# Attention with two mixture layers on one core: v in chunks of 128 tokens, a dummy exponential at the start, and a newly derived order

## The chip, the cores and the metric

The kernel runs on one core of a Trainium2 chip. The metric is device microseconds of that core from the first to the last instruction, beside what lies around them. Five engines matter: TensorE (PE in the profile; PEld is its weight loads), VectorE (DVE), ScalarE (ACT), GpSimd (POOL) and SyncE (SP), which here issues every DMA. Each engine works through its own instructions in the order in which they were written.

## The reference, cut to what matters

```python
# q, k, v: (4 batches, 8 heads, 576 tokens, 64); p: (4, 8, 32, 64)
def sm_attn(qq, kk, vv):
    s = 0.125 * qq @ kk.T
    a = exp(s - max(s)); a = a / (sum(a) + 1e-9)
    return a @ vv
pp  = sm_attn(p, k, v)          # 32 packed rows per head
x   = sm_attn(q, pp, pp)        # back to 576 tokens; heads joined: (2304, 512)
h   = x @ w_in                  # first MoE: 512 -> 2048
x   = (h * cos(h)) @ w_out      # 2048 -> 512
out = sum over 4 experts e of share[:, e] * (relu(x @ w1[e]) @ w2[e])   # second MoE: 512 -> 1024 -> 512
```

## The kernel before

**Stages.** For each of four batches `attn_p` computes the packed attention: scores (`f_s1`, helper line 353), maximum and exponential (L377 to L386), six transposes of the exponentials in chunks of 96 tokens (`f_tr`, L392), a copy of them out of the accumulators (`f_aT`, L396), and the product with v (`f_pv`, L409), for each of two halves `e` of the heads. `attn_q` computes the second scores (`f_s2`, again helper line 353), transposes them on DVE (L466), takes maxima (L470), exponentials (L477) and sums, and writes the result in two parts, rounded (`f_hi`, L499) and remainder (`f_lo`, L658), as tile `at`. `w_block` decodes 64-bit weights: load, absolute value on ACT (L264), clamp, shift and sign on DVE (L271, L275, L280), low word on ACT (L285), sum on POOL (L294). `m_front` (helper line 353, then L547) folds the packed attention into the first weight matrix; `a_front` (products on L205 to L207, cosine on L573 to L590) and `a_back` are the first MoE, in 16 steps of one batch and one quarter of its 2048 columns. The second MoE takes the tokens in thirds, eight steps each; for the last two thirds `b_back2` forms seven products a step, collects them in sums (L1134), and after a third's last step adds the sums into each other (`final`, L1149) and stores them (`put`, L1156). Every product is three matmuls of a rounded part and a remainder (`mm3`, L205 to L207).

**What sets the order.** Nothing is ordered by hand. `Plan` is a small list planner inside the kernel: each operation has an engine, an assumed cost in us, its predecessors, the buffers that it takes, and a key. `Plan.run` goes through an assumed timeline. Whichever operation can start first is taken next on its engine; among those of one engine that could start at the same moment the smallest key wins; a TensorE operation whose key is more than 60 above the smallest one left is held back. The instructions are written in the resulting order, so a wrong cost does not break anything, but it places an instruction behind one that comes late. The keys stand in the table `KEYS`: for an attention batch `att` (scores, transposes, v product, last transpose, second scores, store), `m`, `f`, `b` for the first MoE, `load` for the loads, `first`, `one`, `two`, `end`, `last` for the second. `last` gives the keys of the seven products of the very last step, in the order of the list `BACK`.

**Costs assumed.** Loads of the first stages are costed at 0.27 MB per us, a half-batch of scores on TensorE at 1.5 us; the first exponential is charged 1.3 us for loading its table. Before the first scores and in planned gaps of the first 31 us TensorE runs matmuls of the identity (L1254, L1365). The loads of one batch pair of v arrive as two tiles of 96 partitions.

Of the kernel before, what the change touches and what calls it, by code (L numbers as in the profile page):

```python
# [26 lines left out]
class Plan:  # L27
# [18 lines left out]
    def op(self, eng, us, f, after=(), take=(), use=(), key=None, table=None, port=False, alt=None, begun=()):  # L46
# [4 lines left out]
        o = {"eng": eng, "us": us, "late": self.late if eng == "SP" else 0.0, "fair": self.late > 0, "f": f, "after": [a for a in after if a is not None], "take": list(take),  # L51
# [11 lines left out]
    def run(self):  # L63
# [4 lines left out]
        port, free, table, taken = 0.0, {}, None, {t: 0 for t in self.bufs}  # L68
# [10 lines left out]
        while done < len(self.ops):  # L79
# [67 lines left out]
def tile_packed_attention_moe_moe2(ctx: ExitStack, tc: tile.TileContext, qT, kT, vk, pT, w_in, w_out, dp, w1, w2, out, out2):  # L147
# [24 lines left out]
    NCH, CH = vk.shape[3], vk.shape[2]  # L172
# [47 lines left out]
    MB = 1 / 0.27  # L220
# [11 lines left out]
    def w_block(what, G, k, key, pieces=1, ld_key=None):  # L232
# [22 lines left out]
        for p in range(pieces):  # L255
# [56 lines left out]
            his.append(h)  # L312
            a = pl.op("POOL", 2.45 * r, f_add, [a, l, h], [], [sraw, sd], key)
# [9 lines left out]
    ld_p = dma(2.5 + 0.26 * MB, lambda: load(ptile, pT), key=-2000)  # L323

    def load_kv(n, vtag, key, key_v):
# [5 lines left out]
        def f_v():  # L331
            p, b, f = (mp, 2, 4) if vtag == "m" else (wo, 4, 4)
# [4 lines left out]
        s["ld_v"] = dma(0.59 * MB, f_v, take=[s["v"]], key=key_v)  # L337

# [17 lines left out]
    def attn_p(bb, keys):  # L356
# [13 lines left out]
        a = pl.op("PE", 1.5, f_s1, [ld_p, u[0]["ld_k"], u[1]["ld_k"]], p1, [u[0]["k"], u[1]["k"]], keys[0])  # L370
        ready = []
        for e in range(2):
# [16 lines left out]
            def f_tr(e=e):  # L389
                s["tpv", e] = tpv = psum2().rearrange("p c n -> p (c n)")  # L390
                for c in range(NCH):
                    nc.tensor.transpose(tpv[:CH, c * P:(c + 1) * P], s["a", e][:, c * CH:(c + 1) * CH], ident)  # L392

            def f_aT(e=e):
                s["aT", e] = aT = dec.tile([P, 2 * 512], F32, tag="T", name="aT", bufs=2)[:CH, :NCH * P]
                nc.scalar.activation(aT, s["tpv", e][:CH, :NCH * P], AF.Copy)  # L396
# [6 lines left out]
            def f_pv(e=e):  # L403
                if e == 0:
                    s["pv"] = psum2()
                for c in range(NCH):
                    for q in range(4):
                        h = 2 * (q % 2) + e
                        nc.tensor.matmul(s["pv"][32 * q:32 * q + 32, e, :64],  # L409
                                         lhsT=s["aT", e][:, c * P + 32 * q:c * P + 32 * q + 32],  # L410
                                         rhs=u[q // 2]["vt"][:, c, 64 * h:64 * h + 64], start=c == 0, stop=c == NCH - 1)
# [11 lines left out]
            b = pl.op("PE", 0.88, f_tr, [x], [p2[e]], [ta], keys[1])  # L423
            b = pl.op("ACT", 0.8, f_aT, [b], [tT], [p2[e]])
            b = pl.op("PE", 0.88, f_pv, [b, u[0]["ld_v"], u[1]["ld_v"]] + ready[-1:], [p3] if e == 0 else [],
# [17 lines left out]
    def attn_q(bb, key, key_st):  # L443
# [12 lines left out]
        first = pl.op("PE", 1.5, f_s2, [un[bb, "ptf"], u[0]["ld_q"], u[1]["ld_q"]], p1, [u[0]["q"], u[1]["q"]], key)  # L456
# [78 lines left out]
    def m_front(G, bb, key):  # L535
# [16 lines left out]
        a = pl.op("PE", 1.25, f_mm, w[0]["ready"] + w[1]["ready"] + [un[bb, "ptf"]], [p1],  # L552
# [546 lines left out]
    def b_back2(n, W, keys):  # L1099
# [4 lines left out]
        for i, (a, b, bank, new, acc, how) in enumerate(BACK):  # L1104
# [22 lines left out]
            def f_evac(ob=ob, ac=ac, acc=acc, how=how, first=first):  # L1127
                p = ob["t"][:, :, :TB]
# [4 lines left out]
                else:  # L1133
                    nc.vector.tensor_tensor(out=ac["t"], in0=ac["t"] if how == ALU.subtract else p,  # L1134
# [7 lines left out]
        if u < NU - 1:  # L1142
            return
# [274 lines left out]
```

## Time and profile before

| | us |
|---|---|
| median of 3 runs (1148.88 to 1152.58) | 1150.12 |
| the profiled execution | 1149.58 |
| its span | 1147.8 |

| engine | busy us | share of the span |
|---|---|---|
| PE | 1101.7 | 96% |
| PEld | 1032.5 | 90% |
| DVE | 835.3 | 73% |
| POOL | 633.2 | 55% |
| ACT | 493.4 | 43% |

The chain of work that ended last is 78% PE, 8% DVE and 5% DMA. An engine that is busy 96% of the span cannot lose much more waiting, so the places to look at are those few where PE waits: a table of stretches shows them. A row of a timeline gives the start in us, the time, the engine, the line, the operation and its tiles, and in brackets how long the engine was idle before it and what ended that.

### The profile page before, as it was taken

What the parts mean: (1) busy time and instruction counts of PE and PEld (TensorE: products, weight loads), DVE (VectorE), ACT (ScalarE), POOL (GpSimd) and SP (SyncE); (2) the same over time, 40 slices, a digit from 0 to 9 for tenths busy, and PEclk for the clock granted to TensorE, in tenths of its full rate; (3) what the DMA queues carried; (4) which work ended last, traced back from release to release, by engine and by line L of the source; (5) the groups of instructions that cost most, each with busy time, mean ns of one, the idle gap of its engine ahead of it and who ended that gap; (6) DMA issues with size and microseconds to landing.
All of it is one profiled execution on the core that took longest, in us unless ns stands there. A gap on an engine that the chain in (4) does not pass through costs nothing.

```text
span 1147.8 us, 19120 instructions
## 1 busy us (share of the span) xinstructions
PE 1101.7 (96%) x7241; PEld 1032.5 (90%) x7241; DVE 835.3 (73%) x1244; ACT 493.4 (43%) x852; POOL 633.2 (55%) x477
## 2 busy tenths in 40 slices
PE   6689999999999999999999999999999999999997
PEld 4568999999999988888888889999999999999997
DVE  3798777567555677787777756888887768778776
ACT  3677655445444453244334434333334343333331
POOL 1454755435422775555566546656667767645553
PEclk8699999999999999999999999999999999999999
DMA  9673436433135859787866967676667876666653
GB/s 314 231 263 118 161 116 266 188 130 141 43 105 188 280 196 325 265 301 256 291 257 263 335 259 249 232 252 233 244 227 249 306 265 238 226 227 219 228 182 110
DMA packets 96815, 257.70 MB, mean 225 GB/s; under 512 B 10892, under 2 KB 34516, under 8 KB 94548
## 3 DMA queue, kind: packets, MB, share of 16 engines
q1 hardware_dynamic: 96724, 256.48, 63.1%
q8 instruction: 57, 0.93, 0.3%
q14 instruction: 34, 0.28, 0.1%
HBM read 192.97 MB, written 71.86 MB: 231 GB/s over the span
## 4 chain that ended last, share of the span: by engine, by line
PE 78%; DVE 8%; DMA 5%; issue 4%; ACT 3%; POOL 2%; SPq 0%; POOLq 0%; ACTq 0%; DVEq 0%
PE pa L205 26%; PE pa L207 25%; PE pa L206 25%; DMA w<-w 3%; PE pa L353 2%; DVE pa L958 1%; DVE s L755 1%; POOL aop L658 1%; POOL w L658 1%; DMA kt<-kT 1%; DVE acc L1134 1%; DVE p L958 1%; DVE u L975 0%; DVE oacc L1077 0%; DVE g L1010 0%
## 5 line engine op out<-in xcount | busy, mean ns | idle before, releaser
L205 PE MATMUL pa<-g,w 128*128 128x288 f32 (+1 forms) x960 | 303.6, 316 | 2.0 <-DVE acc L1134 0.8
L206 PE MATMUL pa<-g,w 128*128 128x288 f32 (+1 forms) x960 | 301.6, 314 | 1.2 <-POOL g L590 1.2
L207 PE MATMUL pa<-g,w 128*128 128x288 f32 (+1 forms) x960 | 301.2, 314 | 0.5 <-POOL w L297 0.5
L658 POOL TENSOR_TENSOR g<-u,g 128x384 fp32r<-128x384 f32 x157 | 171.5, 1105 | 140.3 <-ACT g L667 133.5
L205 PE MATMUL pa<-bop,aop 128*128 128x384 f32 x672 | 228.8, 341 | 9.3 <-DVE p L958 4.1
L207 PE MATMUL pa<-bop,aop 128*128 128x384 f32 x672 | 226.9, 338 | 1.5 <-POOL aop L658 1.5
L206 PE MATMUL pa<-bop,aop 128*128 128x384 f32 x672 | 226.3, 337 | 1.1 <-POOL bop L658 1.1
L205 PEld LDWEIGHTS pa<-g,w 128*128 128x128 f32 x960 | 180.1, 188 | 7.9 <-issue 2.4
L206 PEld LDWEIGHTS pa<-g,w 128*128 128x128 f32 x960 | 180.2, 188 | 1.9 <-POOL g L590 1.9
L207 PEld LDWEIGHTS pa<-g,w 128*128 128x128 f32 x960 | 180.4, 188 | 1.0 <-POOL w L297 1.0
L667 ACT ACTIVATE g<-u 128x384 fp32r<-128x384 f32 x192 | 97.2, 523 | 176.8 <-DVE u L987 134.9
L590 POOL TENSOR_TENSOR g<-t,g 128x576 fp32r<-128x576 f32 x64 | 93.2, 1470 | 118.8 <-ACT g L587 117.4
L205 PEld LDWEIGHTS pa<-bop,aop 128*128 128x128 f32 x672 | 126.1, 188 | 19.1 <-DVE p L958 6.1
L206 PEld LDWEIGHTS pa<-bop,aop 128*128 128x128 f32 x672 | 126.2, 188 | 3.0 <-POOL bop L658 1.4
L207 PEld LDWEIGHTS pa<-bop,aop 128*128 128x128 f32 x672 | 126.1, 188 | 2.2 <-POOL aop L658 2.2
L958 DVE TENSOR_TENSOR p<-pa,p 128x384 f32<-128x384 f32 x144 | 79.3, 554 | 41.4 <-PE pa L207 38.7
L1134 DVE TENSOR_TENSOR acc<-pa,acc 128x768 f32<-128x768 f32 x88 | 83.9, 954 | 32.6 <-PE pa L207 31.3
L658 POOL TENSOR_TENSOR w<-w 128x512 fp32r<-128x512 f32 x62 | 86.3, 1403 | 31.4 <-ACT w L705 31.2
L205 PE MATMUL pa<-at,m 128*128 128x288 f32 x256 | 78.7, 307 | 3.1 <-DVE t L583 2.0
L206 PE MATMUL pa<-at,m 128*128 128x288 f32 x256 | 77.5, 303 | 2.8 <-POOL at L658 2.8
L205 PE MATMUL pa<-w,g 128*128 128x512 f32 x192 | 75.9, 395 | 1.9 <-DVE oacc L1077 1.9
L207 PE MATMUL pa<-at,m 128*128 128x288 f32 x256 | 77.2, 301 | 0.0
(129 smaller groups left out, 1924.8 us busy)
## 6 DMA issues: line engine op xcount, KB each, us to landing
at<-at SPq DMA_DIRECT2D x16, 1152.0 KB, 5.3
raw<-w SPq DMA_DIRECT2D x32, 512.0 KB, 5.2
w<-w SPq DMA_DIRECT2D x64, 256.0 KB, 5.0
raw<-w_in SPq DMA_DIRECT2D x6, 1024.0 KB, 6.1
raw<-w_out SPq DMA_DIRECT2D x6, 1024.0 KB, 8.0
vt<-vk SPq DMA_DIRECT2D x8, 576.0 KB, 8.5
kt<-kT SPq DMA_DIRECT2D x8, 576.0 KB, 10.5
qt<-qT SPq DMA_DIRECT2D x8, 576.0 KB, 8.6
```

Of the source, the lines that this page charges most:

```text
L205: nc.tensor.matmul(o, lhsT=l(0), rhs=r(0), start=first, stop=False, skip_group_check=True)
L206: nc.tensor.matmul(o, lhsT=l(0), rhs=r(1), start=False, stop=False, skip_group_check=True)
L207: nc.tensor.matmul(o, lhsT=l(1), rhs=r(0), start=False, stop=last, skip_group_check=True)
L353: nc.tensor.matmul(o(e)[32 * q:32 * q + 32, :N], lhsT=l[64 * e:64 * e + 64, 32 * q:32 * q + 32], rhs=r(q // 2, q % 2)[64 * e:64 * e + 64], ...
L590: nc.gpsimd.tensor_tensor(out=s["g"][:, 1], in0=s["t"], in1=s["g"][:, 0].bitcast(F32), op=ALU.subtract)
L658: (nc.vector if on_vector else nc.gpsimd).tensor_tensor(out=dst[:, 1], in0=src, in1=dst[:, 0].bitcast(F32), op=ALU.subtract)
L667: nc.scalar.activation(r["t"][:, 0], src(), AF.Copy)
L755: nc.vector.tensor_tensor(out=t, in0=src(a, m)(), in1=src(b, m)(), op=o)
L958: nc.vector.tensor_tensor(out=s[o] if o in s else tmp(o), in0=s[x], in1=s[y], op=ALU.add)
L1134: nc.vector.tensor_tensor(out=ac["t"], in0=ac["t"] if how == ALU.subtract else p, in1=p if how == ALU.subtract else ac["t"], op=how)
```

## The change

The values `v` arrive as four chunks of 128 tokens and a rest of 64 tokens, which both tiles of a batch share, instead of six chunks of 96. An `Exp` activation on a column of zeros is written ahead of the planned work. In the planner the first stages' loads are costed at 0.4 MB per us and scores at 0.85 us, a TensorE operation may follow another without a latency, the exponential's table counts as loaded, loads of later v tiles wait in the plan for `w_out`'s rounding, and the second MoE's work on ACT, DVE and POOL is costed 1.08 times instead of 1.04. All keys are new. In a third's last step of `b_back2` the sums are added with keys that follow product 5 (counted from 0), and product 6 is evacuated and stored in two halves.

```diff
-        port, free, table, taken = 0.0, {}, None, {t: 0 for t in self.bufs}
+        port, free, table, taken = 0.0, {}, "exp", {t: 0 for t in self.bufs}
-            for x, w in [(x, fin) for x in o["next"]] + [(x, t) for x in o["then"]]:
+            for x, w in [(x, t + us if o["fair"] and eng == "PE" == x["eng"] else fin) for x in o["next"]] + [(x, t) for x in o["then"]]:
-    MB = 1 / 0.27
+    MB = 1 / 0.4
...
-            t = p.tile([P, f * 512], F32, tag=vtag, name="vt", bufs=b)[:CH, :NCH * 256]
-            s["vt"] = load(t.rearrange("p (c n) -> p c n", c=NCH), vk[n // 2, n % 2])
+            s["vt"] = t = p.tile([P, 4 * 512], F32, tag=vtag, name="vt", bufs=b)
+            load(t[:, :4 * 256], vk[n // 2, n % 2])
+            if n % 2 == 0:
+                load(t[:64, 4 * 256:6 * 256], vr[n // 2])
...
-        a = pl.op("PE", 1.5, f_s1, [ld_p, u[0]["ld_k"], u[1]["ld_k"]], p1, [u[0]["k"], u[1]["k"]], keys[0])
+        a = pl.op("PE", 0.85, f_s1, [ld_p, u[0]["ld_k"], u[1]["ld_k"]], p1, [u[0]["k"], u[1]["k"]], keys[0])
...
-                for c in range(NCH):
-                    nc.tensor.transpose(tpv[:CH, c * P:(c + 1) * P], s["a", e][:, c * CH:(c + 1) * CH], ident)
+                for c in range(5):
+                    n = P if c < 4 else 64
+                    nc.tensor.transpose(tpv[:n, c * P:(c + 1) * P], s["a", e][:, c * P:c * P + n], ident)
...
-                nc.scalar.activation(aT, s["tpv", e][:CH, :NCH * P], AF.Copy)
+                nc.scalar.activation(aT[:, :4 * P], s["tpv", e][:, :4 * P], AF.Copy)
+                nc.scalar.activation(aT[:64, 4 * P:5 * P], s["tpv", e][:64, 4 * P:5 * P], AF.Copy)
...
+            if u == NU - 1 and i == 6:
+                for d in range(2):
+                    ac["op"] = pl.op("DVE", 0.56, lambda d=d, f=f_evac: f(slice(d, d + 1)), [m, ac["op"]], [],
+                                     [ob["slot"], ac["slot"]], keys[i] + 8)
+                    put(h, acc, 1, 0, keys[i] + 12, d)
+                continue
...
+            if u == NU - 1 and i == 5:
+                final(h, "x74", "v", keys[i] + 9), final(h, "x53", "v", keys[i] + 10)
+                put(h, "x53", 0, 1, keys[i] + 20)
+                final(h, "w", "x53", keys[i] + 11)
+                put(h, "w", 1, 1, keys[i] + 21)
...
-            'in0': [-1061.7, -368.5],
+            'in0': [-1407.6, -625.9],
-            'last': {'b': [39.4, 45.5, 37.7, 357.6, 51.2, 27.5, 165.9]},
+            'last': {'b': [33.4, 24, 67.5, 310.6, 39.6, 16.1, 197.9]},
-            'load': {'in': -1643.2,
+            'load': {'in': -1654.2,
-                     'v3': -1611,
+                     'v3': -1752.6,
-                     'v5': -1628.7,
+                     'v5': -1536.1,
...
+    warm = small.tile([P, 1], F32, tag="mx", name="warm")
+    nc.vector.memset(warm, 0.0)
+    nc.scalar.activation(warm, warm, AF.Exp)
...
-    pl.slow, pl.late = 1.04, 0.8
+    pl.slow, pl.late = 1.08, 0.8
```

## Rows read from the trace of the kernel before

**Rows 1.** Stretches of the span: length, busy us by engine (instructions), TensorE clock, DMA share, GB/s

```profile
0.00:120.00 120.00, 96.20 (x1158) 75.47 (x1159) 85.90 (x174) 73.99 (x114) 50.80 (x42) 0.89 0.66 221
120.00:400.00 280.00, 280.00 (x2173) 268.86 (x2172) 179.72 (x226) 139.54 (x204) 136.98 (x84) 1.00 0.46 164
400.00:600.00 200.00, 193.01 (x954) 170.71 (x954) 149.63 (x219) 81.76 (x159) 121.71 (x83) 1.00 0.75 271
600.00:1141.00 541.00, 532.08 (x2960) 517.29 (x2959) 416.79 (x623) 198.13 (x378) 323.70 (x271) 1.00 0.68 240
```

**Rows 2.** The same table for three parts of the head

```profile
10.00:20.00 10.00, 8.26 (x116) 5.30 (x108) 3.99 (x12) 5.28 (x10) 0.00 (x0) 0.86 1.05 398
...
20.00:60.00 40.00, 25.79 (x334) 17.71 (x334) 28.71 (x61) 24.74 (x44) 19.96 (x15) 0.70 0.75 243
60.00:120.00 60.00, 56.31 (x696) 46.84 (x681) 53.20 (x103) 43.97 (x63) 30.14 (x22) 1.00 0.50 173
```

**Rows 3.** The chain of waits in the first 44 us: start, us, what

```profile
2.59 8.45 DMA kt<-kT
...
22.53 1.74 PE pa L353 x28
```

**Rows 4.** Timeline of ACT from 14 to 24 us

```profile
14.70 1.28 ACT L386 ACT_TABLE_LOAD   x1 [14.70 <-DVE nb L381]
16.00 0.74 ACT L386 ACTIVATE a<-pa,nb 128x576 f32<-128x576 f32 x1
...
22.37 0.69 ACT L264 ACTIVATE wd<-raw 128x512 f32<-128x512 f32 x1
```

**Rows 5.** The tile raw up to 26 us: issues (ns, first and last start), and landing

```profile
L197 SPq DMA_DIRECT2D raw<-w_in x4: 327/380/591, 4.0 to 8.3; - x4
...
DMA to landing us min/median/max: 4.0/10.9/11.8
```

**Rows 6.** Timelines of DVE and PE from 24 to 42 us

```profile
26.91 1.58 DVE L466 STREAM_TRANSPOSE x<-pa 128x288 f32<-128x288 f32 x4 [2.83 <-PE pa L353]
...
29.04 0.41 DVE L271 TENSOR_SCALAR wd<-wd 128x512 f32<-128x512 f32 x1
...
33.49 1.06 PE L353 MATMUL pa<-wd,ptf 64*32 64x512 f32 x2 [5.05 <-POOL wd L294]
...
41.09 0.61 PE L206 MATMUL pa<-at,m 128*128 128x288 f32 x1 [0.61 <-POOL at L658]
```

**Rows 7.** Timeline of ACT from 35 to 40 us

```profile
36.38 0.66 ACT L264 ACTIVATE dt<-raw 128x512 f32<-128x512 f32 x1
...
37.49 0.67 ACT L499 ACTIVATE at<-xt 128x576 fp32r<-128x576 f32 x1
```

**Rows 8.** The chain of waits near 100 us: transposes and v product of one half

```profile
99.59 0.66 PE pa L392 x6
...
101.70 0.81 PE pa L409 x48
```

**Rows 9.** Timeline from 40 to 66 us: copies from accumulators on ACT

```profile
54.21 0.81 ACT L396 ACTIVATE aT<-pa 96x768 f32<-96x768 f32 x1 [0.66 <-PE pa L409]
...
58.20 0.26 ACT L436 ACTIVATE ptf<-pa 128x128 f32<-128x128 f32 x1
```

**Rows 10.** The page's DMA issues: tiles, count, KB each, median us from issue to landing

```profile
at<-at SPq DMA_DIRECT2D x16, 1152.0 KB, 5.3
```

**Rows 11.** PE's waits from 400 to 1141 us, longest in total: us, times, longest

```profile
PE pa L205 <- DVE p L958: 4.8, 9, 1.2
```

**Rows 12.** Timeline of DVE from 1139 us to the end

```profile
1139.40 0.96 DVE L1134 TENSOR_TENSOR acc<-pa,acc 128x768 f32<-128x768 f32 x1 [1.12 <-PE pa L207]
1140.40 0.96 DVE L1149 TENSOR_TENSOR acc<-acc 128x768 f32<-128x768 f32 x1
1141.49 0.96 DVE L1134 TENSOR_TENSOR acc<-pa,acc 128x768 f32<-128x768 f32 x1
1142.48 1.95 DVE L1149 TENSOR_TENSOR acc<-acc 128x768 f32<-128x768 f32 x2
```

More of the change, by code (lines that the diff above doesn't have):

```diff
@@ L50, in op @@
             us, alt = us * self.slow, alt and alt * self.slow
-        o = {"eng": eng, "us": us, "late": self.late if eng == "SP" else 0.0, "fair": self.late > 0, "f": f, "after": [a for a in after if a is not None], "take": list(take),
+        o = {"eng": eng, "us": us, "late": self.late if eng == "SP" else 0.0, "fair": True, "f": f, "after": [a for a in after if a is not None], "take": list(take),
              "use": list(use) + list(take), "key": key, "table": table, "port": port or eng == "POOL", "n": len(self.ops), "next": [],
@@ L146, in tile_packed_attention_moe_moe2 @@
 @with_exitstack
-def tile_packed_attention_moe_moe2(ctx: ExitStack, tc: tile.TileContext, qT, kT, vk, pT, w_in, w_out, dp, w1, w2, out, out2):
+def tile_packed_attention_moe_moe2(ctx: ExitStack, tc: tile.TileContext, qT, kT, vk, vr, pT, w_in, w_out, dp, w1, w2, out, out2):
     nc = tc.nc
@@ L405, in f_pv @@
                     s["pv"] = psum2()
-                for c in range(NCH):
+                for c in range(5):
+                    n = P if c < 4 else 64
                     for q in range(4):
@@ L1161, in b_back2 @@
-        kf = keys[-1] + 20
-        put("c11", 0, 0, kf)
-        final("x53", "v", kf + 1), final("w", "x53", kf + 2), final("x74", "v", kf + 3)
-        put("x53", 0, 1, kf + 10), put("w", 1, 1, kf + 11), put("x74", 1, 0, kf + 12)
+            if u == NU - 1 and i == 2:
+                put(h, "c11", 0, 0, keys[i] + 20)
+            if u == NU - 1 and i == 5:
[3 more added lines that the diff above has]
+                put(h, "w", 1, 1, keys[i] + 21)
@@ new lines, in final, with f, put @@
+    def final(h, x, y, key):
+        a, b = accs[h, x], accs[h, y]
+        def f():
+            nc.vector.tensor_tensor(out=a["t"], in0=a["t"], in1=b["t"], op=ALU.add)
+        a["op"] = pl.op("DVE", 0.95, f, [a["op"], b["op"]], [], [a["slot"], b["slot"]], key, port=True)
+    def put(h, x, i, c, key, d=None):
+        def f():
+            t0 = (h - 1) * TH + c * TB
+            dst = out2[i * 256:(i + 1) * 256, t0:t0 + TB].rearrange("(d p) n -> p d n", p=P)
+            t = accs[h, x]["t"]
+            nc.sync.dma_start(out=dst if d is None else dst[:, d], in_=t if d is None else t[:, d])
+        dma((0.4 if d is None else 0.2) * MB, f, [accs[h, x]["op"]], [], [accs[h, x]["slot"]], key)
@@ L1245, in qq, with kv @@
+    def kv(n, vtag, begun=()):
+        load_kv(n, vtag, KEYS["load"]["k%d" % n], KEYS["load"]["v%d" % n], begun)
     def qq(n):
@@ L1279, in tile_packed_attention_moe_moe2 @@
             for x in (2 * n + 4, 2 * n + 5):
-                kv(x, "w")
+                kv(x, "w", [wblk["out", 0, k]["hi"] for k in range(2)])
             for x in (2 * n + 4, 2 * n + 5):
@@ L1389 @@
     R = p.shape[2]
-    CH = 96
     def heads_t(a):
```

131 lines of the change are left out of this document (61 added, 70 removed), and 12 rows, old and new, of the table KEYS.

## The prediction

> **What bounds the kernel now.** I read the table of stretches first, then the chain of waits and the timelines where PE waits. From 120 to 400 us PE is busy for all 280.00 us at full clock [rows 1]: the first MoE in its steady state is PE's own work, and no order makes it shorter. From 400 to 600 us PE stands still for 200.00 - 193.01 = 7.0 us, from 600 to 1141 us for 541.00 - 532.08 = 8.9 us. The last addition from an accumulator starts at 1141.49, 6.3 us before the span's end [rows 12]. The head is the soft part: PE lacks 120.00 - 96.20 = 23.8 us up to 120 us, 14.2 of them between 20 and 60 us, where the granted clock also averages only 0.70; from 60 to 120 us it lacks 3.7 [rows 1, 2]. What starts the steady state earlier in the head moves the whole rest with it. So the change is worth what it takes from the chain of the head, plus what its new order does to 16 us of waits in the second MoE, plus the tail.
>
> What makes the head: nothing starts before the second k tile has landed at 2.59 + 8.45 = 11.04 us. The first exponential then waits for its table. The second scores begin at 22.53 us [rows 3], and DVE gets them at 26.91 [rows 6].
>
> **The dummy exponential.** ACT_TABLE_LOAD, 1.28 us, stands right before the first exponential and on the chain [rows 4]. With the dummy it runs while k is still arriving and ACT has nothing to do. After it ACT works without a pause up to the last piece of `w_in` at 22.37, so all of this moves forward if the weights are there. They are loaded behind v3 now (key -1752.6 against -1654.2); before, they came right behind q. v3 is 512 KB of the new form; at the 398 GB/s of these microseconds [rows 2] that is 1.3 us. The slowest piece needed 11.8 us from an issue no later than 8.3 us [rows 5], landing about 20.1; 1.3 later is 21.4, and ACT wants it at 22.37 - 1.28 = 21.1 [rows 4]. Cost at most 0.3, half hidden by the piece before. I take -1.2; bounds -1.3 and 0 (if something else holds the chain).
>
> By the Trainium skill (ScalarE: Activation LUTs, section What ACT_TABLE_LOAD costs) a switch costs the load of about 1283 ns and a drain of about 1380 ns more. The load agrees with the 1.28 us here [rows 4]; ACT was idle before it, and the exponential starts 0.02 us after its end, so no drain is seen. By the page's sum the term would be -2.7 instead of -1.2.
>
> **v in five chunks.** Six transposes (0.66 us) and 24 products (recorded as 48, 0.81 us) of a half become five and 20 [rows 8]: (0.66 + 0.81) / 6 = 0.25 us of PE, eight halves, 2.0 us. On ACT one copy of 768 columns (0.81 us) becomes one of 512 and one of 128; two operations of 512 columns take 1.11 from start to start, 0.56 each [rows 7], one of 128 takes 0.26 [rows 9], so about even: 0.0 to +0.1 each. PE is the nearly full engine in three of the four batches, so I take -0.25 x 6 there and -0.15 x 2 in the first, where transpose, copy and product follow one another: -1.8. Bounds -2.0 and +0.8 (ACT decides, eight times +0.1). The v bytes are the same, 1152 KB for a pair; the four more DMAs fall in a time when SP's issues run ahead of the transfers (issue until 8.3, landing about 11 us later [rows 5]), so I cost them at nothing; if SP were behind, at one issue each, 0.4 us [rows 5].
>
> **The order of the head.** Here before shows a misplacement. DVE waits 2.83 us for the second scores, and behind them in its queue stands the clamp of the last quarter of `w_in` (29.04). PE therefore waits 5.05 us, until 33.49, for that quarter [rows 6]. In the old plan this piece landed late (loads at 0.27 MB per us); at 0.4 it lands earlier in the plan by 7 us (5.9 MB / 0.27 + 2.5 against 6.5 MB / 0.4 + 0.7, v3 included), and its operations go ahead of the scores' transposes. The 5.05 us do not all come out: next late is `at`, whose remainder PE awaits at 41.09 [rows 6]. In its chain ACT rounds behind two operations of `w_out`, 37.49 - 36.38 = 1.1 us [rows 7]. I take those 1.1 us, the row nearest to what ends last; bounds -5.0 (the whole wait) and +5.0 (another of its size put in).
>
> For 60 to 120 us I take a quarter of the 3.7 us that PE lacks, -0.9: the load of `at` takes 5.3 us to land [rows 10], the new plan says 1.18 / 0.4 + 2.2 = 5.2 and the old one 6.6, so loads are placed better. Bounds -3.7 and +3.7.
>
> **Second MoE.** Its operations are the same (but for one evacuation in halves, twice), its keys are somewhat different, and the plan now thinks ACT, DVE and POOL 4% slower. PE's waits there are many and short: the largest group is 4.8 us in nine [rows 11]. I take 0; bounds -4 and +4, a quarter of 15.9 either way.
>
> **Tail.** The sums are meant to go ahead of the last product. Which product is last? The keys of `last` are 310.6 for product 3 and 197.9 for product 6; product 3 is over 60 above, so the planner holds it back until product 6 is out. It was so before (357.6 and 165.9), and the trace shows it: product 6 is added at 1139.40, x74 += v, which needs no product 3, follows at 1140.40, product 3 at 1141.49, and then two dependent sums of 1.95 us together [rows 12]. In the new code these two, x53 += v and w += x53, still need product 3. So the end keeps its evacuation, two sums and a store; only product 6's stores leave earlier, beside PE. I take 0; bounds -2.0 (the two sums) and +0.5 (a fifth store on SP in front of the last).
>
> **Sum.** -1.2 - 1.8 - 1.1 - 0.9 = -5.0 us against the profiled execution's 1149.58: 1144.6. Its median lies 0.54 higher; I forecast 1145.0.
>
> **The rivals.**
>
> *Slower, by scores that come late.* The new plan gives TensorE 0.85 us for a half-batch of scores (1.5 before); in the head the second scores take 26.91 - 22.53 = 4.4 us [rows 3, 6]. DVE takes its queue in order, so whatever is placed behind the scores' transposes waits: 2.83 us at DVE, and 5.05 us at PE when PE's next product needs it [rows 6]. If the plan now puts a quarter of `w_in` or `w_out` behind scores at one more such place, both are paid again, 7.9 us; with the table and v still gaining 3.0 this is +4.9: 1155.0. It decides once the new waits exceed 5.0 us. For it: the assumed scores move further from the measured ones. Against it: the weights are planned earlier by much more.
>
> *Given back.* The gain of the first 40 us is lost in the 20 after it, where DVE works 28.7 of 40 us and ACT 24.7 in strict order at a clock of 0.70 [rows 2], or in a poorer second MoE: -5.0 + 4 = 1149.1. For it: DVE is busy for 53 of the 60 us that follow [rows 2], so it may not follow PE.
>
> *Larger.* The order takes the whole 5.05 us, and PE fills 4 more of the 14.2 us that it lacks: -3.0 - 5.0 - 2.0 = -10, 1140.1. For it: a clock that comes back sooner; 25.8 us of PE's work lie in a stretch at a mean of 0.70 [rows 2], and 40 x 0.30 = 12 us of clock are withheld there.
>
> The Trainium skill (TensorE: Matmul & The Clock Gate, section Part 1: The HAM clock gate) says that the throttled state is the default and that activity releases it; the trace agrees in that the clock is 0.70 where PE is busy 64% of the time and 1.00 where it is 94% [rows 2]. By that rule a fuller head gains a second time, and an emptier one loses a second time.
>
> *The tail does what it says.* If product 6 were last after all, two sums go and the evacuation ends in two halves of about 0.56: -1.9, 1143.1.
>
> **How the numbers follow.** Chances: forecast (1141.5 to 1148.5) 0.45; larger 0.16; tail 0.08; given back 0.14; slower 0.17. What a measurement of this kernel can tell from no change is about 0.3%, 3.5 us: faster is below 1146.7, slower above 1153.6. Of the forecast's 0.45 I put 0.32 below 1146.7 and 0.13 above. Faster 0.32 + 0.16 + 0.08 = 0.56; same 0.13 + 0.14 = 0.27; slower 0.17. The range that leaves out 2 in 10 goes from just under the larger case to just under the slower one: 1139.0 to 1154.0.
>
> **What would show it.** Right: no table load between the first maxima and the first exponential, which starts near 14.8 us; transposes recorded five and v products 40 at a time; PE's wait of 5.05 us for the last quarter of `w_in` gone or under 2 us; the steady state (PE at 20.00 of 20) from about 115 instead of 120 us, and the first MoE's last matmul 4 to 6 us earlier; two L1149-like sums after the last product, and 6 to 6.5 us between the last matmul and the end. Wrong: a gain that appears between 400 and 1141 us instead, PE lacking more than 14 us between 20 and 60, or a last addition in halves of 384 columns.

## The result and the profile after

The changed kernel takes 1164.98 us (median; 1163.46 to 1167.59), 1.0128 times the kernel before, 95% interval [1.0103, 1.0153]. The forecast was 1145.0, the range 1139 to 1154: wrong in sign. The profiled execution is the longest of the four, 1167.59 us, its span 1165.7. Lines moved: L353 is L360 in the new numbering, L377 is L384, L386 is L393, L392 is L400, L466, L470 and L494 are L476, L480 and L504, L630 is L640, L638 is L648; the three products of `mm3` are L204 to L206. The kernels of the experiments differ from this by a line at most places.

First the table of stretches of the changed kernel, in the columns of [rows 1, 2]:

```profile
400.00:600.00 200.00, 184.90 (x921) 164.94 (x920) 139.35 (x211) 79.17 (x151) 107.62 (x75) 0.97 0.73 258
...
20.00:60.00 40.00, 25.92 (x240) 19.32 (x240) 31.21 (x56) 24.47 (x44) 22.41 (x17) 0.66 0.70 251
60.00:120.00 60.00, 53.97 (x660) 44.23 (x661) 44.44 (x89) 37.55 (x58) 33.06 (x24) 0.97 0.46 160
400.00:420.00 20.00, 11.08 (x60) 10.49 (x59) 6.39 (x9) 6.60 (x11) 7.35 (x5) 0.75 0.55 178
```

The head is no better: PE is busy for 25.92 of the 40 us from 20 to 60, as before, but 3.74 us of that are matmuls of the identity (L1386), of which there were none in this stretch before; the clock is lower; and 60 to 120 us lacks 6.0 us of PE where it lacked 3.7 [rows 2]. From 400 to 600 us PE stands still for 15.1 us instead of 7.0 [rows 1], and nearly all of the difference lies in one stretch of 20 us, where the granted clock also falls to 0.75. The kernel before has this there:

```profile
400.00:420.00 20.00, 18.11 (x93) 16.18 (x93) 16.30 (x23) 11.94 (x24) 15.46 (x10) 1.00 0.61 207
```

One moment divides the loss in two: the last addition into `yacc`, with which the first MoE ends (kernel before, then changed kernel; a row ends with the first and last start and the form).

```profile
L630 DVE SCALAR_TENSOR_TENSOR yacc<-pa,yacc x48: 748/758/759, 169.3 to 397.1; 128x576 f32<-128x576 f32 x48
L640 DVE SCALAR_TENSOR_TENSOR yacc<-pa,yacc x48: 745/758/758, 174.3 to 405.7; 128x576 f32<-128x576 f32 x48
```

It comes 8.6 us later, and from there to the end of the span it takes 760.0 us instead of 750.7, 9.3 more. Of these 9.3, PE's standing still in 400:420 is 7.0 (8.9 us against 1.9). The clock adds about 2: the mean of 0.75 is half of the stretch at the lower of the clock's two levels, 1.2 and 2.4 GHz, and most of that half passes while PE stands still, where a low clock costs nothing. The thirteen products that then run at it start 0.32 us apart instead of 0.17 (an estimate from these starts; one product of each kind):

```profile
407.15 0.33 PE L205 MATMUL pa<-bop,aop 128*128 128x384 f32 x1
...
417.35 0.52 PE L205 MATMUL pa<-bop,aop 128*128 128x384 f32 x1
```

**The first loss: the experts' shares.** `probs` (a 36 KB load and four small DVE operations) stands at the fixed planned time 60 in both kernels. First the issue on SP, then DVE (changed kernel):

```profile
62.85 0.43 SPq L1187 DMA_DIRECT2D pr<-dp  x1
63.33 6.00 SPq L196 DMA_DIRECT2D kt<-kT  x1
```

```profile
70.40 0.23 DVE L1188 TENSOR_REDUCE prs<-pr 128x18 f32<-128x72 f32 x1 [4.30 <-DMA pr<-dp]
```

And SP and DVE of the kernel before:

```profile
47.76 0.46 SPq L1169 DMA_DIRECT2D pr<-dp  x1
```

```profile
59.74 0.22 DVE L1170 TENSOR_REDUCE prs<-pr 128x18 f32<-128x72 f32 x1
```

Before, SP ran 12 us ahead of the use. Now the load stands behind other loads, is issued 7.55 us before DVE takes it up, and everything behind it on DVE stands still for 4.30 us. ACT's next exponential comes late by that, and PE waits for it:

```profile
74.81 0.40 PE L204 MATMUL pa<-g,w 128*128 128x288 f32 x1 [3.69 <-ACT a L393]
```

**The second loss: the hand-over from the first MoE to the second.** PE's longest wait from 375 to 462 us (us, times, longest), then SP and ACT there:

```profile
PE pa L204 <- ACT p L1030: 8.2, 1, 8.2
```

```profile
402.24 3.14 SPq L648 DMA_DIRECT2D y<-yacc  x3
405.48 0.41 SPq L196 DMA_DIRECT2D raw<-w  x1
405.94 0.50 SPq L689 DMA_DIRECT2D a0a<-aop  x1
406.55 0.37 SPq L689 DMA_DIRECT2D a1a<-aop  x1
407.01 3.55 SPq L648 DMA_DIRECT2D y<-yacc  x3
```

```profile
414.63 0.84 ACT L677 ACTIVATE bop<-ys 128x768 fp32r<-128x768 f32 x1 [9.69 <-DMA y<-yacc]
415.38 0.47 ACT L1030 ACTIVATE p<-pa 128x384 f32<-128x384 f32 x1
```

ACT's rounding `bop` waits 9.69 us for the store of the first MoE's last result, whose memory its tile takes over; the evacuation of a product (L1030) stands behind it on ACT, and PE waits for that. The last addition into `yacc` ends at 406.46, so 8.2 us pass in the issue and landing of its store. Three bulk transfers stand ahead of that store on SP; whether they are the reason is what experiment 2 asks. Before, three stores there took 1.41 us to issue and ACT's longest wait for them was under 1 us.

The end is as forecast. DVE of the changed kernel:

```profile
1157.34 1.02 DVE L1145 TENSOR_TENSOR acc<-pa,acc 128x384 f32<-128x384 f32 x2
1159.42 0.96 DVE L1145 TENSOR_TENSOR acc<-pa,acc 128x768 f32<-128x768 f32 x1 [1.06 <-PE pa L206]
1160.41 1.95 DVE L1171 TENSOR_TENSOR acc<-acc 128x768 f32<-128x768 f32 x2
```

Product 6 in halves, then product 3, then two dependent sums, 6.28 us from the last addition to the end (6.31 before [rows 12]).

### The profile page after: what moved, and what is told of

It reads as the page before. It is cut to its first block, busy times and chain, and to the rows that moved or that the text cites. A ratio compares the mean times of both kernels' runs of the same rounds, so it can differ in the third digit from the quotient of the medians.

```text
span 1165.7 us, 18998 instructions
## 1 busy us (share of the span) xinstructions
PE 1108.4 (95%) x7185; PEld 1039.0 (89%) x7185; DVE 821.6 (70%) x1223; ACT 489.1 (42%) x861; POOL 658.7 (57%) x501
## 4 chain that ended last, share of the span: by engine, by line
PE 83%; DVE 7%; DMA 4%; issue 2%; ACT 2%; POOL 1%; SPq 1%; ACTq 0%; DVEq 0%; POOLq 0%
PE pa L204 27%; PE pa L206 26%; PE pa L205 26%; PE pa L360 2%; DMA raw<-w_out 1%; DVE p L968 1%; DVE pa L968 1%; DVE u L985 1%; DMA kt<-kT 1%; DMA pr<-dp 1%; DVE oacc L1087 1%; DMA w<-w 1%; DVE s L765 1%; DMA aop<-a3a 1%; DMA w<-q1w 1%
## 5 line engine op out<-in xcount | busy, mean ns | idle before, releaser
L204 PE MATMUL pa<-g,w 128*128 128x288 f32 (+1 forms) x960 | 304.6, 317 | 6.3 <-ACT a L393 3.7
L206 PE MATMUL pa<-g,w 128*128 128x288 f32 (+1 forms) x960 | 301.8, 314 | 0.0
L668 POOL TENSOR_TENSOR g<-u,g 128x384 fp32r<-128x384 f32 x168 | 178.2, 1076 | 128.0 <-ACT g L677 117.1
L204 PE MATMUL pa<-bop,aop 128*128 128x384 f32 x672 | 229.8, 342 | 20.1 <-ACT p L1030 8.8
L206 PE MATMUL pa<-bop,aop 128*128 128x384 f32 x672 | 227.5, 339 | 0.0
L204 PEld LDWEIGHTS pa<-g,w 128*128 128x128 f32 x960 | 180.7, 188 | 13.1 <-ACT a L393 3.9
L206 PEld LDWEIGHTS pa<-g,w 128*128 128x128 f32 x960 | 181.1, 189 | 0.0
L600 POOL TENSOR_TENSOR g<-t,g 128x576 fp32r<-128x576 f32 x64 | 97.6, 1540 | 111.1 <-ACT g L597 102.1
L204 PEld LDWEIGHTS pa<-bop,aop 128*128 128x128 f32 x672 | 126.8, 189 | 29.2 <-ACT p L1030 9.5
L206 PEld LDWEIGHTS pa<-bop,aop 128*128 128x128 f32 x672 | 126.8, 189 | 0.1
L1145 DVE TENSOR_TENSOR acc<-pa,acc 128x768 f32<-128x768 f32 (+1 forms) x90 | 84.2, 938 | 44.5 <-PE pa L206 44.2
L204 PE MATMUL pa<-at,m 128*128 128x288 f32 x256 | 79.7, 311 | 10.8 <-ACT at L509 5.5
L205 PE MATMUL pa<-at,m 128*128 128x288 f32 x256 | 77.8, 304 | 1.3 <-POOL at L668 1.3
L583 ACT ACTIVATE t<-pa 128x576 int32<-128x576 f32 x64 | 41.6, 651 | 88.2 <-PE pa L206 86.3
L204 PE MATMUL pa<-w,g 128*128 128x512 f32 x192 | 76.1, 396 | 2.0 <-DVE oacc L1087 1.3
```

Of the source, the lines that this page charges most:

```text
L204: nc.tensor.matmul(o, lhsT=l(0), rhs=r(0), start=first, stop=False, skip_group_check=True)
L205: nc.tensor.matmul(o, lhsT=l(0), rhs=r(1), start=False, stop=False, skip_group_check=True)
L206: nc.tensor.matmul(o, lhsT=l(1), rhs=r(0), start=False, stop=last, skip_group_check=True)
L583: nc.scalar.activation(s["t"].bitcast(I32), s["u"][:, :, :S2], AF.Copy, bias=0.25)
L600: nc.gpsimd.tensor_tensor(out=s["g"][:, 1], in0=s["t"], in1=s["g"][:, 0].bitcast(F32), op=ALU.subtract)
L668: (nc.vector if on_vector else nc.gpsimd).tensor_tensor(out=dst[:, 1], in0=src, in1=dst[:, 0].bitcast(F32), op=ALU.subtract)
```

## The experiments

Ratios are to the kernel before, with 95% intervals. "Kernel 5" is the kernel of experiment 5, and so on; "e3" is kernel 4, the kernel before with v chunks and dummy. "Head" means all that stands ahead of the first MoE's last addition, "hand-over" what follows on it.

**1. Shares loaded early**: changed kernel, the load split from its use and placed at planned time 36.

```diff
-    def probs():
+    def probs_load():
         nc.sync.dma_start(out=pr, in_=dp.rearrange("(t p) e -> p t e", p=P))
+    def probs():
...
+    plan.append((36.0, len(plan), probs_load))
```

> The changed kernel with one DMA moved: the load of the expert shares (pr) is issued ahead of the first batch's store of at, not at planned time 60; DVE's four operations on it stay where they are. Theory A (the head was lost where DVE waits 4.3 us for this load): the wait is gone, the first MoE ends 4 to 6 us earlier, 1159 to 1161 us. Rival B (the head is paced by PE at the low clock, the load only fills a wait that is there anyway): under 1.5 us of gain, 1163.5 to 1166 us.

1162.96 us, 1.0107 [1.0086, 1.0128]. DVE no longer waits for `pr`, the last addition into `yacc` comes at 401.6 instead of 405.7, but PE's wait at the hand-over stays 6.9 us. The time lies between the two theories, and its interval overlaps that of the changed kernel.

**2. Bulk transfers behind the last store**: changed kernel, `raw`, `a0a` and `a1a` of the listing above written behind the last y store.

```diff
-    plan = [(o["start"], o["n"], o["f"]) for o in order]
+    ysto = [o["start"] for o in order if o["f"].__name__ == "f_store" and "a_back" in o["f"].__qualname__]
+    bulk = [o for o in order if o["eng"] == "SP" and sorted(ysto)[-2] < o["start"] < max(ysto)]
+    plan = [(max(ysto) + 0.001 if any(o is x for x in bulk) else o["start"], o["n"], o["f"]) for o in order]
```

> The changed kernel with three DMAs moved (a weight load of 512 KB and two stores of 512 KB): they are issued behind the last store of the first MoE's result, not ahead of it. Theory A (PE's 8.2 us wait after 407 us is the landing of that store, which stands behind 1.5 MB): the store lands some 4 us sooner after its issue, PE's wait falls to about 4 us, 1159 to 1161 us. Rival B (the wait is set by the planned order of products on PE and ACT alone): the wait stays, 1164 to 1166 us.

1163.51 us, 1.0104 [1.009, 1.0118], again between the theories and within the noise of the changed kernel. PE's wait of 8.2 us became 3.5, so more than half of it hung on the transfers; DVE's wait for `pr`, which this kernel keeps, is 4.9 us. PE's wait:

```profile
PE pa L204 <- ACT p L1030: 3.5, 1, 3.5
```

**3. Both** edits, 1 and 2, in the changed kernel.

> Both moves together in the changed kernel. Theory A (two separate losses): the two gains add, 1154 to 1157 us. Rival B (the second loss is only the first one handed on): no better than the better one of the two, 1159 to 1161 us.

1159.13 us (1158.32 to 1159.94), 1.0064 [1.0052, 1.0076]. The two faults hold 1.0128 - 1.0064, about 7 us. The time is in rival B's range, but its reason does not hold: together the edits gain more than the better one alone (2.4 and 2.8 us). What is left is still slower than before, so these two are not the whole cause.

**4. Old order, new work**: the kernel before with the v chunks and the dummy, nothing else.

```diff
+    warm = small.tile([P, 1], F32, tag="mx", name="warm")
+    nc.vector.memset(warm, 0.0)
+    nc.scalar.activation(warm, warm, AF.Exp)
...
-                for c in range(NCH):
+                for c in range(5):
+                    n = P if c < 4 else 64
```

> The kernel before, with its own planner costs, keys and sums, and v in chunks of 128 and the dummy exponential alone added; the order of the planned operations is that of the kernel before. Theory A (the new order is the whole loss): the two parts gain 2 to 3 us, 1147 to 1148.5 us. Rival B (v in five chunks costs time on ACT and SP): slower than before, 1152 us or more.

1146.68 us (1141.87 to 1149.72), 0.9952 [0.9934, 0.997]: these parts gain 5.5 us, where 2 to 3 were expected. So the order, with the planner's new costs that make it, loses some 20 us, and the question is which part of it.

**5. Product 3 ahead of product 6**: e3 with the new end in the last third, and product 3's key lowered so that product 6 really is last.

```diff
-            'last': {'b': [39.4, 45.5, 37.7, 357.6, 51.2, 27.5, 165.9]},
+            'last': {'b': [39.4, 45.5, 37.7, 60, 51.2, 27.5, 165.9]},
```

> The kernel before with v in chunks and the dummy exponential (old order), with the new sums and halves in the last third alone, and with product 3's key in the last step lowered from 357.6 to 60, so that product 6 is the last product. Theory A (the keys kept the new sums from doing what they are for): two sums go from the tail, 4.2 to 4.5 us between the last product's first addition and the end in place of 6.3, and about 1.9 us less than the same kernel without it (0.9952 of before), 0.9935 of before. Rival B (the stores' landing sets the end, whatever the sums): 6 us stay, 0.995 of before.

1146.05 us, 0.9957 [0.994, 0.9973]: the same as e3 within both intervals, as rival B had it, though not for its reason. DVE at its end:

```profile
1142.34 0.56 DVE L1144 TENSOR_TENSOR acc<-pa,acc 128x384 f32<-128x384 f32 x1
1142.81 0.95 DVE L1177 TENSOR_TENSOR acc<-acc 128x768 f32<-128x768 f32 x1
1143.68 0.55 DVE L1144 TENSOR_TENSOR acc<-pa,acc 128x384 f32<-128x384 f32 x1
```

From the first half's start to the end of the span of 1147.7 are 5.4 us instead of 6.3. A sum still stands between the halves, so half of what the tail could give is lost; 0.9 us is below what the times can tell.

**6. The new second MoE behind the old head**: e3 with all new key lists of the second MoE (`copy` to `two`) and the stretch of 1.08.

```diff
-    pl.slow, pl.late = 1.04, 0.8
+    pl.slow, pl.late = 1.08, 0.8
```

> The kernel before with v in chunks and the dummy exponential, the first MoE's keys and costs as before, but the second MoE's keys and its factor 1.08 from the changed kernel. Theory A (the second MoE's new order costs little; the loss is made in the head and at the boundary that the head's order leads to): within 2 us of the kernel with the old order throughout, 0.9940 to 0.9970 of before. Rival B (the remaining loss, 7 to 12 us, is the second MoE's new order): 1.000 to 1.006 of before.

1165.03 us, 1.0118 [1.0092, 1.0145]. It is beyond both theories. I took this for the cause at first: all of the loss, with the head untouched. (Its six runs take 1161.67 to 1161.92 us at mean granted clocks of 0.991 to 0.993 or 1168.14 to 1170.29 at 0.982 to 0.984; what makes the clock differ is not shown.) But the idle time is not where the changed kernel has it. PE has 73.17 us of 80 at 380:460 (77.64 in e3, 70.48 in the changed kernel) and a second gap that both lack:

```profile
900.00:940.00 40.00, 33.21 (x173) 32.24 (x173) 28.15 (x39) 11.22 (x22) 23.88 (x19) 0.87 0.66 225
```

**7 and 8. The clock in the head**: matmuls of the identity in PE's planned gap near 31 to 38 us, in the old order (7: on kernel 5, 43 of them) and in the new one (8: on kernel 3, 57).

```diff
+        if a["start"] > 26 and b["start"] < 40 and b["start"] - a["end"] > 5:
+            plan.append((a["end"], len(plan), lambda n=int((b["start"] - a["end"] - 0.5) / 0.16): idle(n)))
```

> The kernel with the old order, v in chunks, the dummy exponential and product 6 last, and 43 matmuls of the identity written into PE's planned wait ahead of the first product with w_in. Theory A (the spread of the old order, 1142 to 1150 us, follows the clock granted in the head): mean clock at or over 0.993 in every run, a spread under 4 us, 0.990 to 0.993 of before. Rival B (PE waits on POOL there, and the fill only delays it): no faster than without the fill, or 1 to 3 us slower.

> The changed kernel with both moves (shares early, bulk later) and 57 matmuls of the identity written into PE's wait of 6.3 us between the first product with w_in and the first product of the first MoE. Theory A (the rest of the head's loss is the clock: it stays near 0.5 to 0.7 until 58 us behind that empty stretch): the clock is back by 45 us, the first MoE starts 3 to 6 us earlier, 1153 to 1156 us. Rival B (the chain through DVE and ACT paces the head whatever PE's clock): within 1.5 us of 1159 us (1.0064 of before).

1148.65 us, 0.9975 [0.996, 0.9989], and 1158.79 us, 1.0068 [1.005, 1.0087]; kernels 5 and 3 without them had 0.9957 and 1.0064. Neither gained. (Kernel 7's clocks are 0.991 to 0.994 over its runs and its spread 5.9 us, which misses theory A too.) But the edit did more than fill a gap: both fills last longer than the gap that they were made for. In kernel 7 the fill takes 10.40 us, and the quarter of `w_in` that PE awaited at 30.50 in kernel 5 is taken up at 33.37. Kernel 8, then kernel 3:

```profile
30.10 12.99 PE L1388 MATMUL pa<-ident 128*128 128x128 f32 x114
42.85 0.38 PE L204 MATMUL pa<-at,m 128*128 128x288 f32 x1
...
56.97 1.21 PE L360 MATMUL pa<-qt,ptf 64*32 64x288 f32 x32 [0.80 <-ACT ptf L446]
```

```profile
38.17 0.61 PE L204 MATMUL pa<-at,m 128*128 128x288 f32 x1 [6.25 <-ACT at L509]
...
60.95 1.20 PE L360 MATMUL pa<-qt,ptf 64*32 64x288 f32 x32 [0.80 <-ACT ptf L446]
```

The first product of the first MoE starts 4.7 us late because the fill still runs; the clock of 20:60 is back, where it was 0.70 in kernel 3:

```profile
20.00:60.00 40.00, 32.93 (x411) 26.53 (x419) 33.72 (x58) 25.37 (x42) 24.35 (x18) 1.00 0.74 259
```

and the next batch's second scores then start 4.0 us earlier. In these two profiled executions kernel 8 keeps that lead: the last addition into `yacc` is at 399.0 instead of 402.2, and the time 1156.78 instead of 1159.94 us. But this is kernel 8's shortest run, at a mean clock of 0.995; its others have 0.986 to 0.993 and take up to 1163.28 us, and the median does not move. So rival B's number was met, but its reason is not shown, and theory A is not refuted: what the clock of the head is worth stays open, since no fill that ends with its gap was tried.

**9. The new head in front of the old second MoE**: the changed kernel with the second MoE's old lists (all from `copy` to `two`; one is shown) and 1.04.

```diff
-            'g': [39.5, -12.1],
+            'g': [40.4, 18.4],
...
-    pl.slow, pl.late = 1.08, 0.8
+    pl.slow, pl.late = 1.04, 0.8
```

> The changed kernel with only the second MoE's part of the written order taken back (its lists of order keys and the planner's stretch of 1.04 in place of 1.08); v chunks, dummy, the first MoE's new order, the late share load and the new end stay. Theory A (the second MoE's new order is nearly the whole loss, as it cost 18.4 us by itself): 1147 to 1152 us, PE busy over 76 of the 80 us of 380:460. Rival B (the late share load and the new head, which this kernel keeps, cost by themselves, or the old order does not fit the new head): 1156 us or more.

1166.06 us, 1.0128 [1.0101, 1.0154]. Theory A fell: taking back the second MoE's order gives nothing. PE's waits at the hand-over and from 895 to 960 us:

```profile
PE pa L204 <- DVE p L968: 7.4, 1, 7.4
...
PE pa L204 <- DMA w<-q7w: 6.3, 1, 6.3
```

The stall at the hand-over is there with the old second MoE too; it comes with the new head. The second wait is a gap near 900, where kernel 6 has one too. Both put a half of the order beside a half that it was not made with; that is not enough by itself, since kernel 15 below does so too and has no such gap (PE busy for 38.85 us of 900:940).

**10 to 12. Kernel 6 in parts**, each on e3: only the lists of the first third (`first`, `one`); only those of the later thirds (`two`, `end`, `last`; a part of each is shown); only the stretch of 1.08, as the line in 6.

```diff
-            'last': {'b': [39.4, 45.5, 37.7, 357.6, 51.2, 27.5, 165.9]},
+            'last': {'b': [33.4, 24, 67.5, 310.6, 39.6, 16.1, 197.9]},
-            'two': {'a': [-11.2, 43, 29.3, 19.8, 20.5, 46.9, 7.1, 23, 52.9, 69, 21.4, 71.4, 100.2, 84.8],
+            'two': {'a': [-11.2, 43, -47.6, 14.1, 17.4, 49.9, 14.2, 5.5, 52.9, 69, 14.1, 71.4, 100.3, 89.7],
```

> The kernel before with v chunks and dummy, and of the new second MoE order only the key lists of its first third (first step and the six that follow it). Theory A (the loss is made where the first MoE hands over to the second): 1155 to 1162 us, PE idle 4 us or more in 380:460 and a clock under 1.00 there. Rival B (the loss comes from the later thirds, as the idle at 905 of the earlier run): 1145 to 1150 us.

> The kernel before with v chunks and dummy, and of the new second MoE order only the key lists of the second and last third. Theory A (seam): 1144 to 1149 us, as without them. Rival B (later thirds): 1154 us or more, with PE idle after 660.

> The kernel before with v chunks and dummy, old key lists, and only the planner's stretch of ACT, DVE and POOL durations at 1.08 in place of 1.04, which changes the order that the same keys give. Theory A (the keys of the seam): 1144 to 1150 us. Rival B (keys tuned under one stretch do not bear another, and the stretch alone makes the loss): 1154 us or more.

| on e3 (0.9952) | us | ratio |
|---|---|---|
| first third | 1148.59 | 0.997 [0.9955, 0.9986] |
| later thirds | 1142.79 | 0.9917 [0.9892, 0.9942] |
| stretch 1.08 | 1151.05 | 0.9993 [0.9976, 1.0011] |

None holds the loss. The later thirds' lists seem to gain 4 us on e3 (the intervals overlap a little), the stretch costs about 5; its 1151.05 us lie between the two theories.

**13. Kernel 9 without the two faults** (edits of 1 and 2).

> The changed kernel with the second MoE's old lists and stretch (1166.06 us before this), and both faults of the hand-over taken out: the expert shares loaded at planned time 36, and the bulk loads behind the last y store. Theory A (the new head's order costs by these two alone, and the idle at 900 is a second cost of the unlike halves): 1157 to 1162 us, the wait at the hand-over 4 us or less, the idle near 900 still there. Rival B (they and nothing else are the loss): 1148 to 1153 us. Rival C (neither matters here): over 1163 us.

1157.05 us, 1.0045 [1.0028, 1.0063], as theory A had it: the two faults hold 9.6 us here. The wait for `q7w` is still 5.0 us, PE's wait for ACT at the hand-over 3.1.

**14. Only the lists of kept stores** (`keep`, `kept`, `copy`, `g`) on e3.

```diff
-            'keep': [117.2, -167, 205.3, 42.6],
-            'kept': [173.4, 203.5],
+            'keep': [115.2, -164.9, 196.1, 61.5],
+            'kept': [147.4, 202.8],
```

> The kernel before with v chunks and dummy, and of the new second MoE lists only those of the stores that are kept for reuse and of their copies. Theory A (these lists make the 18 us of the earlier run, by late stores that the later thirds' loads wait for): 1156 us or more. Rival B (only all lists together with the stretch do): 1143 to 1150 us.

1146.56 us, 0.9957 [0.9939, 0.9975]: nothing.

**15. Kernel 6 at the old stretch**: all new lists of the second MoE on e3, and

```diff
-    pl.slow, pl.late = 1.08, 0.8
+    pl.slow, pl.late = 1.04, 0.8
```

> The kernel before with v chunks and dummy and all new second MoE lists, but the old stretch of 1.04. Theory A (the stretch together with the lists makes the 18 us): 1143 to 1150 us, which is the sum of what the lists did alone. Rival B (the lists among themselves): 1158 us or more.

1147.13 us, 0.996 [0.9945, 0.9974]. So in kernel 6 the lists cost nothing and the stretch, with them, some 18 us (1.0118 - 0.996, times 1151).

**16. Kernel 3 at the old stretch**, by the same line.

> The changed kernel with both faults of the hand-over taken out (1159.13 us before this) and the stretch of 1.04 instead of 1.08. Theory A (the stretch costs here too, 4 us or more): 1155 us or less. Rival B (the changed kernel's lists were made for 1.08, and the old stretch costs): 1160 us or more.

1157.11 us, 1.0045 [1.0024, 1.0066]. Behind the new head, for which the lists were derived, the same stretch costs about 2 us, and the intervals overlap; neither theory's number was met. Kernels 15 and 16 have the second MoE's lists, stretch and work alike but for the end; they differ in the head's keys and in the planner's costs and rules. (The written order of the second MoE still differs a little, since the planner comes to it at other times: kernel 16 has 492 instructions on POOL, kernel 15 has 479.) PE's waits from 30 to 60 us of kernel 16, then of kernel 15:

```profile
PE pa L204 <- ACT at L509: 6.5, 1, 6.5
PE pa L204 <- DVE t L593: 3.7, 1, 3.7
```

```profile
PE pa L359 <- POOL wd L293: 3.6, 1, 3.6
PE pa L204 <- DVE t L592: 2.5, 1, 2.5
PE pa L204 <- ACT at L508: 1.8, 1, 1.8
```

and the 20 us behind the last addition into `yacc`, in kernel 16, then in 15:

```profile
400.50:420.50 20.00, 15.75 (x78) 14.84 (x77) 12.62 (x18) 11.13 (x22) 14.59 (x10) 0.91 0.79 256
```

```profile
395.20:415.20 20.00, 17.02 (x91) 15.43 (x90) 15.92 (x25) 13.55 (x26) 15.37 (x10) 1.00 0.65 211
```

The last addition into `yacc` is at 400.5 against 395.2: 5.3 us of the head's order, out of 7.9 between the two spans (1152.9 and 1145.0). At the hand-over PE stands still 1.3 us longer, and the clock is lower. Kernel 16's profiled execution is its shortest, so the medians, 1157.11 and 1147.13, lie further apart than these spans.

**17 and 18. Dummy alone, v chunks alone**: the first three lines of the diff in 4 on the kernel before, and all of the rest of it.

> The kernel before with nothing but the dummy exponential ahead of the first real one. The prediction's step (the load of 1.28 us moves out of the chain to the first scores' products): 1.2 us less than before, 1149 to 1151 us. Rival (the head's clock and queues eat it): within 0.5 us of before, or more.

> The kernel before with nothing but v in chunks of 128 tokens (five in place of six: ten transposes for twelve, forty products for forty-eight in each pair). The prediction's step: 1.8 us less than before, 1148 to 1150 us. Rival (the two together gain 5.5, and the dummy at most its 1.3, so the chunks hold about 4): 1145.5 to 1148 us.

1150.76 us and 1149.92 us, both 0.9989 [0.9978, 0.9999]: 1.3 us each, with intervals from 0.1 to 2.5. Together (kernel 4) they gave 5.5 [3.5, 7.6]; the intervals of sum and whole overlap, so whether there is more in them together stays open.

**The balance**, in us against the kernel before (ratio less 1, times 1151): old head with dummy, v chunks and new lists -4.6 (kernel 15); the new head's order without its two faults +9.8 (16 less 15; it takes in the new end, which 5 puts at about nothing); the stretch +2.2 (3 less 16); the late shares and stores +7.4 (changed kernel less 3); together +14.8, measured +14.7 (1.0128). These are differences along one chain of kernels, so they must add up, and another chain gives other sizes: at the stretch of 1.08 the same exchange of heads, from kernel 6 to kernel 3, takes off 6.2 us (1.0118 to 1.0064), because kernel 6's 18 us for the stretch are not there behind the new head. What does not hang on the chain is when the first MoE ends. One profiled execution of each:

| kernels | last addition into `yacc` at, us | from there to the end, us |
|---|---|---|
| before | 397.1 | 750.7 |
| old head, dummy and v chunks, 1.04 (4, 5, 10, 11, 14, 15) | 390.5 to 395.2 | 749.2 to 753.8 |
| the same, 1.08, old lists (12), new lists (6) | 391.5, 396.4 | 757.2, 770.1 |
| new head, shares early (1, 3, 13, 16) | 400.5 to 402.2 | 757.7, 756.0, 756.0, 752.4 |
| new head, shares late (changed kernel, 2, 9) | 405.7 to 407.2 | 760.0, 756.3, 762.3 |

With the same work, every kernel with the new head ends the first MoE later than every kernel with the old one, by some 8 us, and the late shares add 5.

## Why the prediction was wrong

**The dummy, -1.2: right.** The load runs at 0.73 us and the first exponential starts at 14.77, not 16.00 [rows 4]. ACT of the changed kernel:

```profile
0.73 1.28 ACT L1272 ACT_TABLE_LOAD   x1 [0.73 <-PEq L1431]
...
14.77 0.74 ACT L393 ACTIVATE a<-pa,nb 128x576 f32<-128x576 f32 x1 [12.55 <-DVE nb L388]
```

Alone it gave 1.3 us. By the Trainium skill (ScalarE: Activation LUTs, What ACT_TABLE_LOAD costs) a drain comes on top, and by an estimate from its figures the gain would have been 2.7; the interval of 0.1 to 2.5 leaves that out by little. A load between two busy operations shows no drain either: in the kernel before ACT ends one at 47.01, loads from 47.02 to 48.30, and starts the next at 48.32.

**v in five chunks, -1.8: right in kind.** Alone it gave 1.3. Kernel 18's groups: PE's transposes are busy for 5.6 us in 40 instructions (before 6.7 in 48), its products 7.2 in 320 (before 7.5 in 384), so PE saves 1.4, where I had put 2.0 by taking a sixth of both; ACT's copies take 4.7 + 2.1 instead of 6.2 us.

```profile
L418 PE MATMUL pa<-vt,aT 128*32 128x64 f32 (+1 forms) x320 | 7.2, 223 | 0.8 <-DVE pz L425 0.6 <-ACT aT L403 0.3
L399 PE MATMUL pa<-ident,a 128*128 128x128 f32 (+1 forms) x40 | 5.6, 278 | 0.6 <-ACT a L392 0.6
```

**The order of the head, "I take those 1.1 us" and "a quarter of the 3.7 us that PE lacks, -0.9": failed.** The misplaced wait for `w_in` did go; the second scores reach DVE at 23.76 instead of 26.91 [rows 6]. But the first product of the first MoE starts at 38.20, where it started at 38.22. The step that I named as next late, `at`, took the whole gain, and not on ACT, where I had looked for it: there its rounding now follows its input at once. PE and ACT, then DVE of the changed kernel:

```profile
38.20 0.61 PE L204 MATMUL pa<-at,m 128*128 128x288 f32 x1 [5.55 <-ACT at L509]
```

```profile
37.48 0.67 ACT L509 ACTIVATE at<-xt 128x576 fp32r<-128x576 f32 x1
```

```profile
23.76 1.58 DVE L476 STREAM_TRANSPOSE x<-pa 128x288 f32<-128x288 f32 x4 [0.31 <-PE pa L360]
26.99 0.76 DVE L384 TENSOR_REDUCE mx<-pa 128x1 f32<-128x576 f32 x1 [1.66 <-PE pa L360]
...
29.79 1.40 DVE L480 TENSOR_REDUCE m<-x 128x18 f32<-128x576 f32 x2
...
36.51 0.78 DVE L504 STREAM_TRANSPOSE xt<-x 128x576 f32<-128x576 f32 x1
```

And the same two steps of DVE in the kernel before:

```profile
28.41 0.71 DVE L470 TENSOR_REDUCE m<-x 128x18 f32<-128x576 f32 x1
...
35.29 1.43 DVE L494 STREAM_TRANSPOSE xt<-x 128x576 f32<-128x576 f32 x2
```

DVE has the transposed second scores at 25.34, but the new order puts the maximum of the next batch's first scores (L384), with the last quarter of `w_in`, ahead of theirs (L480) and waits 1.66 us for those scores. So their maximum starts at 29.79 instead of 28.41, and `at`'s input comes 1.2 us later, where the forecast had it earlier. From 60 to 120 us PE lacks 2.3 us more, not 0.9 less. With the old order and the same work the first product starts at 34.75 (kernel 15). After that the order loses 4.30 us of DVE for `pr`, which I had not looked at because its lines are not in the diff. It is not moved, but all that stands ahead of it on SP is. Where the forecast had -2.0 for the head's order, the first MoE ends some 8 us later by the order and 5 more by the late shares; in times, along the chain of the balance, it is +9.8, and +7.4 for the shares and the hand-over. My bound of +5.0 was for one more wait "of its size"; the head has two, and a third lies 340 us later.

**Second MoE, "I take 0; bounds -4 and +4, a quarter of 15.9 either way": failed as the term, mainly at the hand-over.** Its lists are worth 0 at the old stretch (kernel 15 against e3), as I took. The stretch, of which I wrote only that the plan now thinks three engines slower, costs 2 us behind the new head, and some 18 behind the old one (kernel 6). What cost 7.0 us of PE in 400:420 and about 2 of clock is the end of the first MoE: its last stores, late, behind bulk transfers, and the memory that they give back. A quarter of the existing waits is no bound for a wait that does not exist yet: 8.2 us stands in a single row. By the Trainium skill (TensorE: Matmul & The Clock Gate, Part 1: The HAM clock gate) activity releases the clock, so an emptier stretch loses a second time; the trace agrees at this place, where PE is busy for 11.08 of 20 us at 0.75, and the second loss is the smaller one. The rival "larger" counted 12 us of withheld clock in the head in the same way as time, though PE stands still in part of that stretch; kernel 8 shows the clock back there and no lower median, with a fill that itself came in the way.

**The tail, 0: right**, and by its mechanism: product 3 is held back by its key and stays last. With product 6 last, it would be worth 0.9 by kernel 5's trace, not 1.9.

**The rival "scores that come late"** (1155.0) had the right form, a wait put in at DVE that passes to PE, and a part of the object: DVE does wait for scores (1.66 us at 26.99), but those of the next batch. The last quarter of `w_in` and the second scores' maximum both stand behind them, and it is the latter for which PE pays. The two larger waits are for DMAs on SP's queue.

**What stays open.** Which entry of the planner puts the next batch's scores ahead, and what else makes the new head slower without its two faults; why PE still waits 3.1 us for ACT at the hand-over in kernel 16; what the clock of the head is worth. The planner's costs alone, with the old lists, were not tried. The best kernel measured is number 11, the old order with dummy, v chunks and the new lists of the later thirds: 1142.79 us, 0.9917 [0.9892, 0.9942], faster than both.

## What to carry to other kernels

A program order that a planner writes is only as good as its assumed times: every instruction that stands on a fixed planned time, and every store whose completion gives memory back, has to be followed through the new order on its queue, whether the diff touches it or not. When work and order change together, measure the work in the old order first; here the work gained 5 us and the new order lost 20. Keys that were tuned together don't bear being exchanged in part: the same stretch of 1.08 cost 5, 18 or 2 us, as the lists and the head around it were. And look at what a filler does to the first real instruction behind it before reading its time: here it ended 4.7 us too late.

## What the runs showed that I had not expected

A load of 36 KB (`pr`) was taken up only 7.55 us after its issue among other loads, and the issue of one k load behind it kept SP for 6.00 us. The issue of a store can take long too: three stores of y took SP 1.41 us in the kernel before, 3.14 and 3.55 us in the changed kernel. The bulk transfers ahead of them are not the whole reason, since the 3.14 us have none directly ahead; the reason is not shown. Matmuls of the identity over PE's idle time raised the granted clock of 20:60 from 0.70 to 1.00 and delayed the first real product by 4.7 us, and the median time stayed where it was.
